# The path for splits with an expert over three tiles, under a second test in place of the other arm

## The chip, the cores and the metric

The kernel runs on one core of a Trainium2 chip. The metric is the device time of one execution in microseconds (us). The page of the profile gives, beside it, the span from the first to the last recorded instruction. The engines are PE (TensorE, matrix products; its weight loads stand as PEld), DVE (VectorE), ACT (ScalarE), POOL (GpSimd) and SP (SyncE, which here issues transfers). Each engine has a sequencer of its own, which reads the engine's instructions in order; the profile marks what the sequencer does itself (branches, semaphore instructions, drains) with a q: PEq or PEldq, DVEq, POOLq and so on.

## The reference

Sliding window attention for 8 batches of 8 heads, 576 positions and 64 dimensions, then a layer of 8 experts with one expert for each token:

```python
def _moe_ref(x, w_gate, w1, w2):            # x: 4608 x 512, from the attention
    logits = x @ w_gate                     # 512 x 8
    expert_idx = np.argmax(logits, axis=1)
    ...
    for e in range(E):                      # E = 8 experts
        lo, hi = (boundaries[e], boundaries[e + 1])
        h = np.maximum(x_sorted[lo:hi] @ w1[e], 0.0)     # 512 x 1024
        y_sorted[lo:hi] = h @ w2[e]                      # 1024 x 512
    y = y_sorted[inv_perm]
    return (gate_w[:, None] * y).astype(np.float32)
```

The number of tokens of an expert is known only when the kernel runs. For the given inputs the eight experts have 669, 400, 748, 505, 592, 390, 566 and 738 tokens.

## The kernel before

**Stages.** The first stage (lines 496 to 1044) is the attention, the choice of experts and the table `perm_i`, which holds for each slot of each tile the token that stands there. A tile is 256 slots (`TB`) of one expert. The last lines of this stage already work on the first two tiles of expert 0, and `loads()` (line 869) puts the numbers of tiles into registers of every engine: `regs[e]` for each expert, `end` (the number of all tiles) and `most` (the largest number of tiles of any expert). The second stage (from line 1054) works on the other tiles. The program is written in the order in which each engine is to run it, since both stages stand under `manual_schedule`.

**A tile.** `gather` fetches the rows of 256 tokens from `x_dram` by two indirect transfers that POOL issues. `hidden` multiplies by the first weights on PE, `output` by the second ones; both use seven products of halves in place of eight, with sums that DVE and POOL form. The last products of `output` write the PSUM banks that `yw2`, `yps[0]` and `yx2` name. `finish` (line 425) is the rest of a tile: three additions on DVE, through the helper `plus` on line 384, of which the first two read `yw2` and the third reads both halves of `yps[0]`. `scatter` (line 291) then sends the tile's 256 rows to their places in `out`: one small copy of the slots into `at_s` on POOL, then two indirect transfers of 256 KB each, `ys[1]` first and `ys[0]` after it. `finish` and `scatter` of a tile do not stand at its own end but at the start of the next one, in `body` (line 479), so that PE has work of the next tile meanwhile. After the last tile they stand by themselves, at line 1126.

**Branches.** `expert(e)` (line 1063) tests for each further tile whether the expert has it (line 1077, `tiles > n`) and whether it is a full one or one of at most 160 tokens (line 1078, `fulls > n`). It is written for at most three tiles of an expert (`KT`). `any_number` (line 1092) is a loop for any split: each turn loads the weights of its tile anew, forms all sums, gathers, multiplies and scatters. Line 1123 chooses between the two by `most`. With the tokens above no expert has more than three tiles, so that the arm with `expert` runs, and no instruction of the loop of line 1104 is in the trace. Each test is a compare and branch on every engine by itself.

**Semaphores.** Engines wait for each other by semaphores that count what an engine has finished; the waits compare with constants. Where two ways through the program come together, both must leave every count at the same value, so the framework puts an instruction into the way with fewer counts that waits for that engine's own last count and adds the difference (EVENT_SEMAPHORE in the rows; INC_SWDGE_SEM for those that POOL's indirect transfers count).

Of the kernel before, what the change touches and what calls it, by code (L numbers as in the profile page):

```python
# [11 lines left out]
F32 = mybir.dt.float32  # L12
# [3 lines left out]
ALU = mybir.AluOpType  # L16
AX = mybir.AxisListType
# [7 lines left out]
def _ins(ap: bass.AP, axis: int, n: int) -> bass.AP:  # L25

    dims = [list(d) for d in ap.ap]
    dims.insert(axis, [0, n])
    return bass.AP(tensor=ap.tensor, offset=ap.offset, ap=dims)


def _inner(ap: bass.AP, n: int) -> bass.AP:
    return _ins(ap, len(ap.ap), n)
# [3 lines left out]
def kernel(  # L37
# [11 lines left out]
    P = nc.NUM_PARTITIONS  # L49
    B, H, S, D = q.shape  # L50
    NT, DM = out.shape
    E = moe_w_gate.shape[1]
# [13 lines left out]
    C = TB // P  # L66
    NE = 2
    NTILE = (NT + TB - 1) // TB + E - 1 + NE
    NX = NTILE + 4
    NS = NX * C  # L70
    KT = 3
# [18 lines left out]
    perm_i = consts.tile([P, NS], I32, name="perm_i")  # L90
# [5 lines left out]
    expert_i = consts.tile([P, NTILE], I32, name="expert_i")  # L96
# [4 lines left out]
    V, G = nc.vector, nc.gpsimd  # L101
# [48 lines left out]
    def sums_w1(e):  # L150
        form(left_sums(G, s1s[e % NW], *w1q(e)))

    def sums_w2(e):
        form(right_sums(G, s2s[e % NW], *w2q(e)))

    def load_w1(e):
        return nc.sync.dma_start(out=w1s[e % NW][:], in_=w1v[e])

    def load_w2(e):
        nc.sync.dma_start(out=w2s[e % NW][:], in_=w2v[e])  # L160
# [7 lines left out]
    lane = consts.tile([P, P], BF16, name="lane")  # L168
# [9 lines left out]
    with tc.tile_pool(name="tmp", bufs=1) as tmp:  # L178
# [8 lines left out]
        for i in range(BG):  # L187
# [12 lines left out]
            out=before[:], in_=ones[:], pattern=[[1, P]], compare_op=ALU.is_gt, fill=0.0, base=0,  # L200
# [6 lines left out]
    nt, cum, start, chunk0 = (consts.tile([P, E], F32, name=n) for n in ("nt", "cum", "start", "chunk0"))  # L207
    rt = ctx.enter_context(tc.tile_pool(name="rt", bufs=1))
# [31 lines left out]
    v_m = Memory(consts.tile([P, 3 * 2 * BG * NV * 2 * VW], F32, name="v_m"))  # L240
# [27 lines left out]
    def form_all(parts):  # L268
        for _ in parts:
            pass  # L270

    def gather(tokens):
        G.tensor_copy(out=at_g[:], in_=tokens)
        for c in range(C):
            G.indirect_dma_start(  # L275
                out=xg[c], out_offset=None, in_=x_dram[:, :],
                in_offset=bass.IndirectOffsetOnAxis(ap=at_g[:, c : c + 1], axis=0),
            )
# [12 lines left out]
    def scatter(tokens):  # L291
        G.tensor_copy(out=at_s[:], in_=tokens)
        for c in reversed(range(C)):

            put = G.indirect_dma_start(  # L295
                out=out[:, :], out_offset=bass.IndirectOffsetOnAxis(ap=at_s[:, c : c + 1], axis=0),
                in_=ys[c], in_offset=None, bounds_check=NT - 1, oob_is_err=False,
            )
            tc.declare_no_dep(put.ins, group="puts", reason="every token has one slot, so no row is written twice")
            tc.add_to_no_dep_group("puts", put.ins)  # L300
# [24 lines left out]
    def keep_turned():  # L325
        for c in range(C):
            nc.scalar.copy(out=xq[:, :, c], in_=xn[:, c])  # L327

    def sums_x(src):

        b12, b22, b21 = src[1][:, 0:HG], src[1][:, HG:], src[0][:, HG:]
        for n, (a, b) in enumerate(((b12, part(0, 0)), (b22, xs[:, 0]), (b22, part(0, 1)), (xs[:, 1], b21))):
            V.tensor_tensor(out=xs[:, n], in0=a, in1=b, op=ALU.subtract)
# [91 lines left out]
    def finish():  # L425

        plus(ys[1][:, hi_], yw2, v3)
        plus(v2, yw2, v1)
        plus(ys[0], yps[0], v02)
# [49 lines left out]
    def body(e, last, after, full, between=None, next_x=True):  # L479

        finish()
        scatter(perm_i[:, last])
        if between is not None:
            between()
        blocks = turned_blocks() if next_x else iter(())
        if not full:
            half_tile(e, blocks, after, next_x)
            return
        form_all(hidden(e, blocks))
        parts = output(e, blocks, next_x)  # L490
        next(parts)
        if after is not None:
            gather(perm_i[:, after])
        form_all(parts)

    with tc.manual_schedule(), ExitStack() as held, ExitStack() as brief:
# [372 lines left out]
        def loads():  # L869

            _, n = nc.values_load_multi_w_load_instructions(info_i[0:1, :], min_val=0, max_val=NT // P)
            _, places = nc.values_load_multi_w_load_instructions(
                places_i[0:1, :], engines=(mybir.EngineType.Pool,), min_val=0, max_val=NTILE,
                skip_runtime_bounds_check_because="sums of numbers of tiles, at most NTILE for any tokens",
            )
            return [(n[e], n[E + e], places[e]) for e in range(E)], places[E], n[2 * E]
# [164 lines left out]
        regs, end, most = loads()  # L1041
# [12 lines left out]
    with tc.manual_schedule():  # L1054
        load_w1(1)
        load_w2(1)
        def at(n):
            n = nc.s_assert_within(
                n, 0, NTILE - 1, skip_runtime_bounds_check_because="a tile with a token is one of the NTILE"
            )  # L1060
            return lambda ahead: bass.ds((n + ahead) * C, C)

        def expert(e):

            fulls, tiles, first = regs[e]
            if 0 < e < E - 1:
                load_w1(e + 1)
                load_w2(e + 1)

            def one(n, full, between=None):  # L1070
                slots = at(first + n)
                ends = e == E - 1 and (n == KT - 1 or not full)
                body(e, slots(0), None if ends or e == E - 1 and n == KT - 2 else slots(3), full, between, not ends)

            def more(n, between=None):

                with tc.If(tiles > n) as some_left:  # L1077
                    with tc.If(fulls > n, preferred_fallthrough_block=False) as full:
                        one(n, True, between)
                        if n + 1 < KT:  # L1080
                            more(n + 1)
                    with full.Else():
                        one(n, False, between)
                if between is not None:
                    with some_left.Else():
                        between()

            if e:
                one(0, True, partial(sums_w2, e))
            more(1 if e else NE, partial(sums_w1, e + 1) if e + 1 < E else None)  # L1090

        def any_number():

            tiles_of = rt.tile([P, E, NTILE], F32, name="tiles_of")
            V.tensor_tensor(
                out=tiles_of[:], in0=_inner(cum[:], NTILE), in1=_ins(lane[:, 0:NTILE], 1, E), op=ALU.is_le
            )
            with nc.allow_low_precision("integers"):
                V.tensor_reduce(out=expert_i[:], in_=tiles_of[:].rearrange("p e t -> p t e"), axis=AX.X, op=ALU.add)
            _, (tiles,) = nc.values_load_multi_w_load_instructions(  # L1100
                places_i[0:1, E : E + 1], min_val=0, max_val=NTILE,
                skip_runtime_bounds_check_because="a sum of numbers of tiles, at most NTILE for any tokens",
            )
            with tc.For_i(NE, tiles) as i:
                _, (e,) = nc.values_load_multi_w_load_instructions(
                    expert_i[0:1, bass.ds(i, 1)], engines=(mybir.EngineType.SP,), min_val=0, max_val=E - 1,
                    skip_runtime_bounds_check_because="a tile that is numbered belongs to an expert",
                )
                for w, view in ((w1s[0], w1v), (w2s[0], w2v)):
                    nc.sync.dma_start(out=w[:], in_=view[bass.ds(e, 1)].rearrange("o p n d -> (o p) n d"))  # L1110
                sums_w1(0)
                sums_w2(0)
                slots = at(i)
                gather(perm_i[:, slots(1)])
                form_all(turned_blocks())
                keep_turned()
                sums_x([xn[:, c] for c in range(C)])
                form_all(hidden(0))
                form_all(output(0, iter(()), False))
                finish()  # L1120
                scatter(perm_i[:, slots(1)])

        with tc.If(most < KT + 1) as few:  # L1123
            for e in range(E):
                expert(e)
            finish()
            scatter(perm_i[:, bass.ds(end * C, C)])
        with few.Else():
            finish()
            scatter(perm_i[:, NE * C : (NE + 1) * C])  # L1130
            any_number()


# [26 lines left out]
```

## Time and profile before

| | |
|---|---|
| runs of the kernel | 721.09, 724.43, 720.25, 723.32 us; median 722.2 us |
| the profiled execution | 721.14 us, its span 719.4 us |
| mean granted clock of TensorE | 0.985 |
| PE busy, 290 to 700 us (second stage) | 408.85 of 410.00 us |
| PE busy, 700 to 719.4 us (the end) | 8.17 of 19.40 us |
| indirect transfers to `out` (line 295) | 42 on POOL, 1.0 us each to issue, median 3.2 us to landing |
| first and last entry of line 1123 | 249.5 us (SP) and 709.0 us (POOL) |

The profile is read on a page (busy time, slices, the chain of waits that ended last) and by questions to the trace: a timeline of the instructions in a stretch, merged where they are alike; and all instructions of one source line, with the shortest, the median and the longest duration in nanoseconds and the times of the first and the last one. A line of the timeline has the start, the duration until the last of the group ends, engine, source line, operation, what is written and read, how many, and in brackets the engine's idle time before it with what ended it. Matrix products are recorded with modelled ends.

### The profile page before, as it was taken

To read this page: it belongs to the slowest core of one execution; us is meant where nothing else is said; L and a number is where in the kernel's file an instruction comes from. 1 tells how busy PE (TensorE), PEld (TensorE's weight loads), DVE (VectorE), ACT (ScalarE), POOL (GpSimd) and SP (SyncE) were. 2 spreads that over 40 slices of the span, in tenths; PEclk is the share of its full clock that TensorE was granted. 3 is DMA by queue.
4 is the path that set the end of the run, shared out by engine and by line. 5 is a ranking of instruction groups with operands and counts; after the bars stand their busy time and mean duration, and the time that the engine had idled before them with its cause. 6 is when DMAs were issued, how large, how long until landed. Compare 5 with 4: busy or idle time off the path is not lost. (4 is left out here: it accounts for less than half of the span.)

```text
span 719.4 us, 17946 instructions
## 1 busy us (share of the span) xinstructions
PE 687.7 (96%) x6882; PEld 606.0 (84%) x6882; DVE 497.7 (69%) x1636; ACT 258.5 (36%) x653; POOL 350.8 (49%) x360
## 2 busy tenths in 40 slices
PE   4999999999979999999999999999999999999993
PEld 3888888878759898897999999899889799889993
DVE  3576899898966858676776686567756677766731
ACT  4688888878745111111121121122111112111110
POOL 4213749387474117857452446545265745272011
PEclk9899999999999999999999999999999999999997
DMA  8998889887442373617101631540361710111000
GB/s 158 221 203 183 178 197 234 205 205 197 123 159 92 104 260 128 215 59 263 51 30 62 199 115 39 192 148 15 124 210 59 269 50 25 61 37 61 2 31 28
DMA packets 137288, 93.37 MB, mean 130 GB/s; under 512 B 117008, under 2 KB 117008, under 8 KB 137170
## 3 DMA queue, kind: packets, MB, share of 16 engines
q1 hardware_dynamic: 127858, 62.16, 32.7%
q0 software_dynamic: 8736, 27.53, 11.8%
q10 hardware_dynamic: 576, 2.10, 1.0%
q8 instruction: 74, 1.21, 0.7%
q14 instruction: 44, 0.36, 0.2%
HBM read 72.89 MB, written 20.45 MB: 130 GB/s over the span
## 5 line engine op out<-in xcount | busy, mean ns | idle before, releaser
L315 DVE STREAM_TRANSPOSE v_m<-qk_m 32x256 f32<-32x256 f32 x304 | 132.4, 435 | 7.9 <-DMA qk_m<-x_dram,at_g 2.3
L344 PE MATMUL bank<-qk_m,s 128*128 128x128 f32 x1024 | 122.5, 275 | 0.2 <-DVE qk_m L365 0.2
L344 PEld LDWEIGHTS bank<-qk_m,s 128*128 128x128 f32 x1024 | 118.3, 192 | 0.4 <-issue 0.4
L275 POOL DMA_INDIRECT qk_m<-x_dram,at_g x38 | 41.0, 1080 | 141.3 <-DVE v_m L315 112.9
L651 ACT ACTIVATE pr<-pr,mx 128x128 f32<-128x128 f32 x288 | 89.6, 390 | 33.6 <-DVE mx L641 33.4
L344 PE MATMUL bank<-qk_m,w 128*128 128x128 f32 x768 | 93.8, 275 | 0.9 <-PEq L1077 0.7
L344 PEld LDWEIGHTS bank<-qk_m,w 128*128 128x128 f32 x768 | 90.6, 192 | 4.5 <-issue 4.1
L295 POOL DMA_INDIRECT out_dram<-v_m,at_s x42 | 42.5, 1011 | 87.5 <-DVE v_m L384 85.2
L641 DVE CUSTOM_DVE_ANT_0 pr<-bank,mask 128x128 f32<-128x128 f32 x288 | 64.3, 285 | 28.4 <-PE bank L628 27.1
L384 DVE TENSOR_TENSOR v_m<-bank,v_m 128x256 f32<-128x256 f32 (+1 forms) x95 | 43.8, 480 | 44.8 <-PE bank L388 30.1
L569 POOL COPY v_m<-v_m 64x520 f32<-64x520 f32 x32 | 19.8, 620 | 68.5 <-DMA v_m<-in_v_dram 58.3
L140 POOL TENSOR_TENSOR s<-w 128x1024 f32<-128x1024 f32 x22 | 52.2, 2374 | 0.0
L674 PEld LDWEIGHTS bank<-v_m,pT 128*64 128x64 f32 x1152 | 41.1, 140 | 11.9 <-DVE xs L688 5.8
L674 PE MATMUL bank<-v_m,pT 128*64 128x65 f32 x1152 | 47.8, 231 | 2.9 <-DVE xs L688 2.9
L351 ACT COPY qk_m<-bank 128x512 f32<-128x512 f32 x16 | 9.4, 587 | 108.7 <-PE bank L344 70.4
L388 PE MATMUL bank<-qkT_m,v_m 128*128 128x256 f32 x216 | 48.3, 379 | 0.0
L388 PEld LDWEIGHTS bank<-qkT_m,v_m 128*128 128x128 f32 x216 | 41.0, 190 | 5.5
L628 PE MATMUL bank<-qkT_m 64*64 64x128 f32 x1152 | 45.4, 287 | 0.2
L595 PE MATMUL bank<-ident,qk_m 128*128 128x128 f32 x256 | 36.8, 287 | 8.8 <-DMA qk_m<-in_q_dram 8.1
L444 PEld LDWEIGHTS bank<-qk_m,w 128*128 128x128 f32 x320 | 43.9, 190 | 0.9 <-issue 0.7
L444 PE MATMUL bank<-qk_m,w 128*128 128x160 f32 x320 | 44.4, 299 | 0.4 <-ACT qk_m L327 0.4
L659 PE MATMUL bank<-ident,pr 128*128 128x128 f32 x288 | 43.0, 287 | 0.0
(174 smaller groups left out, 1229.7 us busy)
## 6 DMA issues: line engine op xcount, KB each, us to landing
w<-in_moe_w_dram SPq DMA_DIRECT2D x11, 2048.0 KB, 9.8
qk_m<-in_q_dram SPq DMA_DIRECT2D x72, 128.0 KB, 3.9
qk_m<-in_k_dram SPq DMA_DIRECT2D x72, 128.0 KB, 3.7
v_m<-in_v_dram SPq DMA_DIRECT2D x64, 128.0 KB, 4.2
qk_m<-in_moe_w_dram SPq DMA_DIRECT2D x3, 2048.0 KB, 10.4
x_dram<-xs POOLq DMA_DIRECT2D x6, 512.0 KB
x_dram<-xs POOLq DMA_DIRECT2D x3, 768.0 KB
w<-in_moe_w_dram ACTq DMA_DIRECT2D x4, 512.0 KB, 4.4
```

Of the source, the lines that this page charges most:

```text
L140: op()
L295: put = G.indirect_dma_start(out=out[:, :], out_offset=bass.IndirectOffsetOnAxis(ap=at_s[:, c : c + 1], axis=0), in_=ys[c], in_offset=None ...
L315: V.transpose(out=xn[b * QD : (b + 1) * QD, :, :, a * QD : (a + 1) * QD].rearrange("p c g i -> p (c g) i"), in_=rows[a * QD : (a + 1) * QD ...
L344: nc.tensor.matmul(acc[:, f, :], lhsT=a[:, g, f * P : (f + 1) * P], rhs=b[:, g, :], start=(first and f == 0 and g == 0), stop=(g == HG - 1 ...
L384: plus = lambda out, a, b: V.tensor_tensor(out=out, in0=a, in1=b, op=ALU.add)
L388: nc.tensor.matmul(acc, lhsT=a[:, f, :], rhs=b[:, f, :], start=(start and f == 0), stop=(stop and f == HF - 1), skip_group_check=True,)
L444: nc.tensor.matmul(acc[:, i], lhsT=w1[:, g, f * P : (f + 1) * P], rhs=xq[:, g].rearrange("p c s -> p (c s)")[:, 0:HALF], start=(i + g == 0 ...
L628: nc.tensor.matmul(out_, lhsT=qT[rows, t, a * WINDOW : (a + 1) * WINDOW], rhs=rhs, start=True, stop=True, skip_group_check=True,)
L641: V.tensor_tensor_reduce(out=prs[h][:, m, :], in0=scs[h][:, m, :], in1=mask[:, m0 + m, :], scale=-scale, scalar=-2 * MASKED, op0=ALU.add, ...
L651: nc.scalar.activation(out=y, in_=y, func=AF.Exp, scale=-1.0, bias=mx[:, h, m : m + 1])
L659: nc.tensor.transpose(out=tr[:, m, :], in_=prs[h][:, m, :], identity=ident[:])
L674: nc.tensor.matmul(px[a * D : (a + 1) * D, h, m, :], lhsT=pTs[h][:, m, a * D : (a + 1) * D], rhs=vt[:, h, :], start=True, stop=True, skip_ ...
```

## The change

`any_number` no longer is the other arm of the first test. The first test has an arm only for splits of at most three tiles an expert. A second test, of the opposite sign, follows it and holds `any_number`; and `finish` and `scatter` of the last tile follow both tests, where both arms had a `finish` and a `scatter` of their own before. In the loop of `any_number`, `finish` and `scatter` of the tile before move from the end of a turn to its start. The table `tiles_of`, which only `any_number` uses, is no longer a tile of 864 bytes a partition in the pool `rt` but a view of the memory `v_m`.

```diff
-            tiles_of = rt.tile([P, E, NTILE], F32, name="tiles_of")
+            tiles_of = v_m(2080, E, NTILE)
...
                 slots = at(i)
+                finish()
+                scatter(perm_i[:, slots(0)])
                 gather(perm_i[:, slots(1)])
                 form_all(turned_blocks())
                 keep_turned()
                 sums_x([xn[:, c] for c in range(C)])
                 form_all(hidden(0))
                 form_all(output(0, iter(()), False))
-                finish()
-                scatter(perm_i[:, slots(1)])
-
-        with tc.If(most < KT + 1) as few:
+
+        with tc.If(most < KT + 1):
             for e in range(E):
                 expert(e)
-            finish()
-            scatter(perm_i[:, bass.ds(end * C, C)])
-        with few.Else():
-            finish()
-            scatter(perm_i[:, NE * C : (NE + 1) * C])
+        with tc.If(most > KT):
             any_number()
+        finish()
+        scatter(perm_i[:, bass.ds(end * C, C)])
```

More of the change, by code (lines that the diff above doesn't have):

```diff
@@ L1092, in any_number @@
         def any_number():
-            tiles_of = rt.tile([P, E, NTILE], F32, name="tiles_of")
+            tiles_of = v_m(2080, E, NTILE)
             V.tensor_tensor(
-                out=tiles_of[:], in0=_inner(cum[:], NTILE), in1=_ins(lane[:, 0:NTILE], 1, E), op=ALU.is_le
+                out=tiles_of, in0=_inner(cum[:], NTILE), in1=_ins(lane[:, 0:NTILE], 1, E), op=ALU.is_le
             )
             with nc.allow_low_precision("integers"):
-                V.tensor_reduce(out=expert_i[:], in_=tiles_of[:].rearrange("p e t -> p t e"), axis=AX.X, op=ALU.add)
+                V.tensor_reduce(out=expert_i[:], in_=tiles_of.rearrange("p e t -> p t e"), axis=AX.X, op=ALU.add)
             _, (tiles,) = nc.values_load_multi_w_load_instructions(
```

## The prediction

> **What bounds the kernel now.** I read the page first: PE works for nearly the whole span, so what counts is what PE waits for, and the piece at the end in which nothing is left for it.
>
> ```profile
> span 719.4 us, 17946 instructions
> ...
> PE 687.7 (96%) x6882; PEld 606.0 (84%) x6882; DVE 497.7 (69%) x1636; ACT 258.5 (36%) x653; POOL 350.8 (49%) x360
> ```
>
> The change moves nothing before the last tile of expert 7, so the next view is the timeline of the end.
>
> ```profile
> 706.28 1.89 PE L388 MATMUL bank<-w,v_m 128*128 128x256 f32 x8
> 706.54 0.76 DVE L384 TENSOR_TENSOR v_m<-bank,v_m 128x256 f32<-128x256 f32 x2 [0.90 <-PE bank L388]
> ...
> 707.75 0.98 POOL L295 DMA_INDIRECT out_dram<-v_m,at_s  x1 [19.93 <-DVE v_m L384]
> 708.21 0.69 DVE L384 TENSOR_TENSOR v_m<-bank,v_m 128x512 f32<-128x512 f32 x1 [0.92 <-PE bank L388]
> ...
> 709.18 0.98 POOL L295 DMA_INDIRECT out_dram<-v_m,at_s  x1 [0.45 <-POOLq L1123]
> ```
>
> The last product runs until 708.17. The first two additions of `finish` start at 706.54, beside it; only the third, at 708.21, needs its end. The first scatter has therefore been issued before the second half is added. After 709.18 there is one thing left, in the rows of line 1155:
>
> ```profile
> L1155 POOLq DRAIN  x3: 46/113/9387, 709.2 to 719.1; - x3
> L1155 SPq DRAIN  x3: 7/7/13, 712.8 to 718.8; - x3
> ```
>
> SP has seen all landings by 712.8; POOL's drain starts at 709.2, with the last scatter, and lasts 9.39 us, and the program ends 0.8 us after it.
>
> Then the branches: the rows of line 1123, and those of line 1077, where an expert with two tiles skips its third.
>
> ```profile
> L1123 PEldq COMPARE_BRANCH  x2: 95/1694/3292, 269.1 to 704.5; - x2
> ...
> L1123 POOLq COMPARE_BRANCH  x2: 37/40/44, 273.3 to 709.0; - x2
> L1123 DVEq COMPARE_BRANCH  x2: 47/54/60, 275.4 to 708.3; - x2
> ```
> ```profile
> L1077 PEldq COMPARE_BRANCH  x14: 68/75/4120, 269.3 to 679.5; - x14
> ...
> L1077 POOLq INC_SWDGE_SEM  x1: 1387/1387/1387, 452.9 to 452.9; - x1
> L1077 DVEq EVENT_SEMAPHORE  x1: 21/21/21, 455.1 to 455.1; - x1
> L1077 PEldq EVENT_SEMAPHORE  x1: 51/51/51, 457.8 to 457.8; - x1
> ...
>   DVE v_m L384: 2.8, 1
> ```
>
> On line 1123 the first branch is the test, the second the jump over the other arm at the end: 3.29 us on PE, some 0.05 on DVE and POOL. The rows of line 1077 hold one skipped body, with the semaphore instructions that make up its counts, and DVE's `finish` waits 2.8 us for PE there. What follows such a skip is what the change will put at the end:
>
> ```profile
> 455.71 1.89 PE L388 MATMUL bank<-w,v_m 128*128 128x256 f32 x8
> 457.90 1.54 DVE L384 TENSOR_TENSOR v_m<-bank,v_m 128x256 f32<-128x256 f32 x3 [2.83 <-PEq L1077]
> ...
> 459.16 1.02 POOL L295 DMA_INDIRECT out_dram<-v_m,at_s  x1 [4.21 <-DVE v_m L384]
> ...
> 460.49 1.00 POOL L295 DMA_INDIRECT out_dram<-v_m,at_s  x1 [0.30 <-issue]
> ```
>
> All three additions run in one piece, after the last product and after PE's semaphore instruction. At 706.54 two of them ran beside it.
>
> **The change part by part.** Removed: the jump over the other arm behind the last scatter, 0.04 us on POOL at 709.0. Nothing waits for it; worth nothing.
>
> Moved: the whole last step, that is three additions on DVE, one copy into `at_s`, the register moves and two indirect transfers on POOL. It moves past the second test on every queue. ACT and SP pass it at once and nobody waits for them: SP's last branch now is at 569.4. POOL's queue has nothing between 687.8, after the copy into `at_s`, and 707.0. It gets the test (0.04), some waits for landed transfers and an INC_SWDGE_SEM (1.39; 1.00 and 1.78 are the other rows); the copy slips from 687.6 to about 689.5, and 17 us of idle time hide that. Without this cover it would cost its 2 us whole.
>
> Added, and on the path: PE's test of `most > KT`, which jumps over the loop's body, then PE's instruction that makes up the counts. `finish` must wait for the count that holds on both ways, so all three additions wait for this instruction, as at 457.90. On DVE itself the jump costs 0.05 (rows above), and DVE is idle from 705.63 to 706.54 anyway.
>
> How late is PE's instruction? Now its sequencer starts the jump at 704.5 and is done 3.29 us later, at 707.8, under matrix products that run until 708.17. The new jump starts after one more short branch (0.07 to 0.34), and skips the same body: one full tile, 168 products and as many weight loads. It ends between 707.89 and 708.16, just under the products still. So PE's end decides, 708.17.
>
> The sum: from the start of PE's semaphore instruction (457.8 in its row, its own 0.05 included) to DVE's first addition at 457.90 it was 0.15 at most: first addition at 708.32. From there the distances of 457.90: first scatter 1.26 later, 709.58; second 1.33 after that, 710.91. Now it is 709.18: **1.73 us later**. Behind it wait SP's last waits and the drain. If the drain is counted from the last scatter or its landing, all of it moves: 721.14 + 1.73 = 722.87 against the profiled execution. That one lies 1.06 below the median of the runs, which is what a new median compares with: 722.2 + 1.73 = **723.9 us**.
>
> Bounds of what the trace does not show. The drain: it moves by 0, if something else sets its end, or by 1.73; its start row (0.01 after the last scatter's) speaks for the second, which I take. PE's jump: 0.07 at least; at most 6.41, the longest branch of line 1078:
>
> ```profile
> L1078 PEldq COMPARE_BRANCH  x19: 67/342/6412, 269.4 to 704.1; - x19
> ```
>
> That one came while weights were loaded, jumping over several bodies; the nearest row, same body and same moment, is 3.29. Moving `tiles_of` shifts later tiles by 864 bytes: no row shows that an address matters (products of line 344 last 275 ns from `s` and from `w`), and `any_number` does not run. Zero.
>
> A rule of the Trainium skill speaks against this step. The row first: 3.29 us for PE's jump, 0.05 for DVE's. The page "Runtime: NRT & Kernel Launch", section "Instruction fetch mechanics", says that a taken branch to code outside the fetched window stops execution until it has come; it gives no time for that. By that rule alone, with the stall wholly on the path, the sum would be 1.73 + 3.29 = 5.0 and the time 727.2; by the rows it is hidden under the products.
>
> **The rivals.** First, no added wait: the framework keeps the exact count for `finish`, and the two additions still run beside the last product. For it: at the joins near 290 and 331 two additions of `finish` start at 290.19 and 330.80, beside the products of line 470 that end at 291.40 and 334.09. Against it: there the way taken was the one with the products, and at 457.90, as here, it was not. Time 722.2, not slower.
>
> Second, clearly slower: the new jump takes as long as the 6.41 row. From 704.7 it ends at 711.1, 2.9 after PE's end; the sum is 1.73 + 2.9 = 4.6 and the time 726.8. It decides as soon as the jump takes over 3.5 us. Against it: the 3.29 at the same place. A join at which all engines wait for each other can't be its cause: at one test ACT branches at 677.5 and DVE at 680.6.
>
> Third, faster: POOL now jumps at 709.0, just before its drain. If the drain's length comes from that jump, with the code in one line it shrinks at most to the landing, 712.8 in place of 718.6: 5.8 less, 1.73 more, 718.1. Against it: POOL's jumps last 0.04, and the drain starts 0.15 after this one.
>
> Fourth, that the change does nothing here, since the loop does not run: only where its code's place and counts don't matter; the time is that of the first.
>
> **How the numbers follow.** Likeliest case 0.70; no added wait (with the fourth) 0.11; long jump 0.13; shorter drain 0.06. The predicted time is 723.9. The runs shown spread by 2 us to either side of their median, so I let a median move by 1: the low end is 722.2 - 1 = 721.2, which leaves out the short drain; the high end is 726.8 with 0.3 of that: 727.1. A change of 0.5% is 3.6 us, about what a measurement of this kernel can tell from none: faster is under 718.6, the third rival, 0.06; slower is over 725.8, the second rival and the likeliest case on a bad median, 0.13 + 0.08 = 0.21; the rest 0.73.
>
> **What would show it.** Right: the three additions of `finish` in one piece from about 708.3, after an idle time that PE's sequencer ends at the line of the second test; on that line a PE branch of about 3.3 us and one EVENT_SEMAPHORE each on PE, DVE and ACT, an INC_SWDGE_SEM on POOL near 688; the scatters at about 709.6 and 710.9; a drain of about 9.4 us; everything before 704 unchanged. Wrong: two additions still at 706.5 (first rival), a PE branch past 708.2 (second), a drain well under 9 us (third), or any shift before 700, which nothing here explains.

## The result, and the profile after

The changed kernel has a median of 723.19 us (52 runs) against 721.48 us (78 runs of the kernel before). The ratio is 1.0027, with a 95% interval from 1.0017 to 1.0036: slower by 1.95 us by this ratio, between 1.2 and 2.6 (the medians themselves differ by 1.71). The forecast was 1.73 us.

The profiled execution of the changed kernel has a span of 725.9 us, 6.5 more than that of before. Most of this is not the change. SP's first branch, which ends the first stage, lies at 249.5 us in the profile of before and at 254.0 in this one, and from there to the end of the last matrix product it is 458.6 and 458.9 us. In the ten profiled executions of this study that first branch lies anywhere between 249.5 and 254.0, and not by kernel: a second profile of the changed kernel has it at 250.3. So the two ends are compared from the last product on. The timeline of the changed kernel's end:

```profile
711.04 1.89 PE L388 MATMUL bank<-w,v_m 128*128 128x256 f32 x8
713.11 1.54 DVE L384 TENSOR_TENSOR v_m<-bank,v_m 128x256 f32<-128x256 f32 x3 [2.72 <-PEq L1126]
714.34 0.98 POOL L295 DMA_INDIRECT out_dram<-v_m,at_s  x1 [21.73 <-DVE v_m L384]
715.63 0.99 POOL L295 DMA_INDIRECT out_dram<-v_m,at_s  x1 [0.30 <-issue]
```

The last product ends at 711.04 + 1.89 = 712.93. All three additions of `finish` now come in one group behind it, at 713.11, where two of them stood beside the product before; what ended DVE's idle time is PE's sequencer on line 1126, the second test. The second scatter starts 715.63 - 712.93 = 2.70 after the product's end (2.71 from the unrounded times); before it was 709.18 - 708.17 = 1.01. The rows of the second test, and those of the program's end, now on line 1154:

```profile
L1126 PEldq EVENT_SEMAPHORE  x2: 51/51/51, 713.0 to 713.1; - x2
...
L1126 POOLq INC_SWDGE_SEM  x1: 2180/2180/2180, 689.8 to 689.8; - x1
...
L1126 PEldq COMPARE_BRANCH  x1: 3482/3482/3482, 709.1 to 709.1; - x1
L1126 DVEq COMPARE_BRANCH  x1: 63/63/63, 710.2 to 710.2; - x1
...
  DVE v_m L384: 2.7, 1
```
```profile
L1154 POOLq DRAIN  x3: 46/113/10342, 714.7 to 725.6; - x3
L1154 SPq DRAIN  x3: 7/7/13, 719.1 to 725.3; - x3
```

PE's jump over the loop starts at 709.1 and lasts 3.48 us, to 712.62, still 0.3 us under the product. PE's semaphore instruction follows at 713.0, and DVE's additions at 713.11. POOL's drain is recorded as longer (10.34 us for 9.39), but it starts at 714.7, 0.9 us before the second scatter; from that scatter's start to the end of the span it is 725.89 - 715.63 = 10.26, and 719.42 - 709.18 = 10.24 before. The drain has moved as a whole, and it goes by the issue of the last scatter, not by its landing: in the ten profiles the end lies 10.23 to 10.26 us behind the issue, and 7.24 to 7.52 behind the landing.

The chain of waits that ended last, in order of time, reaches back to DVE's wait and no further:

```profile
713.03 0.04 DVEq L384
713.07 0.04 issue
713.11 0.44 DVE v_m L384
...
714.34 0.98 POOL out_dram L295
715.33 1.29 POOLq L1154
```

### The profile page after: what moved, and what is told of

Its sections match the earlier page's. It is cut to its first block, busy times and chain, and to the rows that moved or that the text cites. A ratio compares the mean times of both kernels' runs of the same rounds, so it can differ in the third digit from the quotient of the medians.

```text
span 725.9 us, 17956 instructions
## 1 busy us (share of the span) xinstructions
PE 689.7 (95%) x6882; PEld 607.3 (84%) x6882; DVE 497.8 (69%) x1636; ACT 258.4 (36%) x653; POOL 350.8 (48%) x360
```

## The experiments

**Theory and rivals.** The theory is that the last additions wait for the instruction with which PE makes up the counts of the skipped loop, that this instruction can run only behind PE's last product, and that the price of 1.7 us is the lost overlap. The rivals: the price is PE's jump itself; it is the move of `tiles_of` and of all tiles behind it; a common end behind a second test costs in itself, whatever is waited for.

All eight experiments stand in one table, below the kernel before and the changed one. The ratio is to the kernel before. The three columns after it are read from each profile and count from the end of the last product, in us: start of the first of the last three additions, start of the second scatter, end of the span. The last column is PE's branch at the test or join where the loop is passed.

| kernel | ratio, 95% interval | first addition | second scatter | end | PE's branch |
|---|---|---|---|---|---|
| before | 1 | -1.63 | 1.01 | 11.25 | 3.29 |
| changed | 1.0027, 1.0017 to 1.0036 | 0.18 | 2.71 | 12.96 | 3.48 |
| changed, once more | 1.0018, 0.9995 to 1.0040 | 0.18 | 2.70 | 12.96 | 3.40 |
| tests swapped | 1.0055, 1.0035 to 1.0076 | -1.63 | 1.01 | 11.24 | 0.37 |
| short body | 1.0027, 1.0010 to 1.0045 | 0.18 | 2.71 | 12.96 | 0.35 |
| long body | 1.0024, 1.0008 to 1.0040 | 0.19 | 2.71 | 12.96 | 3.36 |
| table back | 1.0018, 1.0001 to 1.0035 | 0.18 | 2.71 | 12.96 | 3.60 |
| other arm kept | 1.0004, 0.9987 to 1.0021 | -1.63 | 1.00 | 11.25 | 3.49 |
| additions in the arms | 1.0015, 0.9992 to 1.0038 | -1.63 | 2.94 | 13.19 | 3.45 |
| two additions in the arms | 1.0007, 0.9987 to 1.0027 | -1.63 | 1.34 | 11.59 | 3.79 |

The ratios are known to some 0.2%, which is the size of the effect; the columns from the profiles agree to 0.02 us where the kernels should, and decide. Three ratios lie below or at the low end of what was expected (table back, additions in the arms, changed once more), though their intervals reach it; the ratio of the swapped kernel lies clear above.

**A shorter jump.** Of the changed kernel:

```diff
-                form_all(hidden(0))
                 form_all(output(0, iter(()), False))
```

> The changed kernel without hidden in the loop of any_number, which does not run with these tokens (the loop's arithmetic is incomplete, the output of this run is not touched by it): 224 PE instructions fewer to jump over. Wait theory: PE's jump at the second test falls from 3.5 us to under 0.5 us, PE's make-up instruction still waits for the last product, the three additions still run in one piece; the ratio stays at 1.0025 to 1.003. Fetch rival (the price is the jump): 1.000 to 1.0005.

PE's branch fell to 0.35 us and nothing else moved: the same 12.96 us, ratio 1.0027. The rows of the second test in this kernel, on its line 1125, show that PE still waits for its products before the semaphore instruction:

```profile
L1125 PEldq EVENT_SEMAPHORE  x2: 51/51/51, 712.2 to 712.4; - x2
...
L1125 PEldq COMPARE_BRANCH  x1: 347/347/347, 708.4 to 708.4; - x1
```

The branch is done at 708.8, the semaphore instruction comes at 712.2, when the last product (end 712.20) is. The price is not the jump. The Trainium skill, page "Runtime: NRT & Kernel Launch", section "Instruction fetch mechanics", says that a taken branch to code outside the fetched window waits for that code. That 224 PE instructions fewer take 3.1 us from the branch would fit this, but no run here shows what lay in the window. What the rows do show is that a branch of 3.48 us which ends before the queued products do costs nothing.

**A longer jump.** `form_all(hidden(0))` stands four times in the loop:

```diff
                 form_all(hidden(0))
+                form_all(hidden(0))
+                form_all(hidden(0))
+                form_all(hidden(0))
                 form_all(output(0, iter(()), False))
```

> The changed kernel with hidden four times in the loop that does not run: 672 PE instructions more to jump over. Wait theory with its cover of 3.5 us: if the jump takes 6.1 to 6.7 us, as the longest ones of line 1078, the end comes 2.6 to 3.2 us later than in the changed kernel, ratio 1.006 to 1.007; if the length of the jump does not matter beyond the next blocks of code and it stays at 3.5 us, 1.0027. Fetch rival: the whole jump counts, 1.008 or more.

The jump stayed at 3.36 us, the end at 12.96. So 672 instructions more do not by themselves make a jump as long as the branches of 6 us on line 1078, and the case that should have shown the cover run out (the 3.5 us and more for which the products queued ahead keep PE busy) did not come about in this kernel. The trace of before has it at another place, a branch of line 1078 between two tiles (its row, then the products around it):

```profile
L1078 PEldq COMPARE_BRANCH  x1: 4080/4080/4080, 379.4 to 379.4; - x1
```
```profile
381.39 1.89 PE L388 MATMUL bank<-qk_m,v_m 128*128 128x256 f32 x8
383.55 2.05 PE L344 MATMUL bank<-qk_m,w 128*128 128x128 f32 x16 [0.27 <-issue]
```

The branch lasts until 383.50, the products queued ahead of it until 381.39 + 1.89 = 383.28, and PE stands still until 383.55. The ten profiles hold eleven such branches behind the same cover of 3.9 us: after the shortest, 3.86 us, PE is idle for 0.02 us, after the longest, 4.17 us, for 0.34. So a stall is paid as far as it outlasts the products.

**The table back.**

```diff
-            tiles_of = v_m(2080, E, NTILE)
+            tiles_of = rt.tile([P, E, NTILE], F32, name="tiles_of")[:]
```

> The changed kernel with tiles_of in its own tile again, so that later tiles lie where they lay before. Wait theory: the move of the table is worth nothing, ratio 1.0025 to 1.003 as the changed kernel. Memory rival (the shift by 864 bytes is what costs): 1.000.

12.96 us again. The move of the table is worth nothing.

**All but the second test.**

```diff
-        with tc.If(most < KT + 1):
+        with tc.If(most < KT + 1) as few:
             for e in range(E):
                 expert(e)
-        with tc.If(most > KT):
+            finish()
+            scatter(perm_i[:, bass.ds(end * C, C)])
+        with few.Else():
             any_number()
-        finish()
-        scatter(perm_i[:, bass.ds(end * C, C)])
+            finish()
+            scatter(perm_i[:, bass.ds(end * C, C)])
```

> All of the change but the second test: any_number with its turned loop and its table in v_m as the other arm of the first test, finish and scatter written in both arms. Wait theory: as before, two additions beside the last product, ratio 0.999 to 1.001. Memory rival: 1.0025 to 1.003.

The end is that of before to 0.01 us, with the turned loop and the moved table in it, and PE's jump of 3.49 us too. The price belongs to the second test with a common end behind it, and to nothing else in the change.

**The additions in the arms.** `finish` moves into both tests, the scatter stays behind them:

```diff
         with tc.If(most < KT + 1):
             for e in range(E):
                 expert(e)
+            finish()
         with tc.If(most > KT):
             any_number()
-        finish()
+            finish()
         scatter(perm_i[:, bass.ds(end * C, C)])
```

> Both tests, finish inside the experts' arm and inside the loop's arm, only the scatter common behind them. The additions keep their old times, the third ends some 0.7 us after the last product; but the scatters now wait for the instruction with which DVE makes up its counts, behind the third addition. Wait theory, for whichever engine's make-up instruction: the first scatter is issued some 0.8 us after that instruction, the second 1.33 us after the first, so the second comes 1.9 to 2.1 us later than before: ratio 1.0025 to 1.003. Rival, only PE's instruction matters: the time of before, 1.000 to 1.0005.

```profile
706.97 0.76 DVE L384 TENSOR_TENSOR v_m<-bank,v_m 128x256 f32<-128x256 f32 x2 [0.90 <-PE bank L388]
708.64 0.69 DVE L384 TENSOR_TENSOR v_m<-bank,v_m 128x512 f32<-128x512 f32 x1 [0.91 <-PE bank L388]
710.25 0.98 POOL L295 DMA_INDIRECT out_dram<-v_m,at_s  x1 [21.81 <-DVEq L1127]
711.54 0.99 POOL L295 DMA_INDIRECT out_dram<-v_m,at_s  x1 [0.30 <-issue]
```

This is the timeline of its end. The additions have the distances of before, and yet the second scatter comes 1.93 us later than before, later even than in the changed kernel: POOL now waits for DVE's sequencer on line 1127, the second test, and DVE's instruction there stands behind the third addition:

```profile
L1127 DVEq EVENT_SEMAPHORE  x2: 21/21/21, 709.4 to 709.5; - x2
```

The wait is not PE's in particular. It is for the make-up instruction of whichever engine is waited for behind the skip.

**Two additions in the arms.** `plus(ys[1][:, hi_], yw2, v3)` and `plus(v2, yw2, v1)` stand inside both tests, `plus(ys[0], yps[0], v02)` and the scatter behind them:

```diff
         with tc.If(most < KT + 1):
             for e in range(E):
                 expert(e)
+            first_two()
         with tc.If(most > KT):
             any_number()
-        finish()
+            first_two()
+        plus(ys[0], yps[0], v02)
         scatter(perm_i[:, bass.ds(end * C, C)])
```

> Both tests, the first two additions of finish inside either arm, the third addition and the scatter common behind them. Wait theory: the two additions run beside the last product again; the third waits for PE's make-up instruction, 0.1 us later than before; the first scatter waits for DVE's make-up instruction, which comes early; the second scatter is at most 0.4 us later than before: ratio 1.000 to 1.001. Rival, a common end behind a second test costs in itself: 1.0025 to 1.003.

```profile
707.74 0.76 DVE L384 TENSOR_TENSOR v_m<-bank,v_m 128x256 f32<-128x256 f32 x2 [0.90 <-PE bank L388]
709.40 0.98 POOL L295 DMA_INDIRECT out_dram<-v_m,at_s  x1 [20.19 <-DVEq L1131]
709.75 0.69 DVE L384 TENSOR_TENSOR v_m<-bank,v_m 128x512 f32<-128x512 f32 x1 [1.25 <-PEq L1131]
710.72 0.98 POOL L295 DMA_INDIRECT out_dram<-v_m,at_s  x1 [0.33 <-DVE v_m L384]
```

The last product ends at 709.38 here. Two additions are beside it again, and the end is 0.34 us later than before, where the changed kernel is 1.71 later. What is left is the third addition, 0.37 after the product in place of 0.04: it waits for PE's make-up instruction, and that came late, because PE's jump was the longest of all here:

```profile
L1131 PEldq EVENT_SEMAPHORE  x2: 51/51/51, 709.7 to 709.8; - x2
...
L1131 PEldq COMPARE_BRANCH  x1: 3786/3786/3786, 705.8 to 705.8; - x1
```

The jump ends at 709.60, 0.23 us behind the last product. So in this kernel, at the very place of the change, a part of the jump is paid: the addition is 0.19 us later than in the changed kernel (0.37 against 0.18). A common end behind a second test costs little in itself; what costs is that waits which were for one exact result before are now for an engine's make-up instruction.

**The tests swapped.**

```diff
+        with tc.If(most > KT):
+            any_number()
         with tc.If(most < KT + 1):
             for e in range(E):
                 expert(e)
-        with tc.If(most > KT):
-            any_number()
         finish()
         scatter(perm_i[:, bass.ds(end * C, C)])
```

> The two tests in the other order: the loop's test first, the experts' test second, finish and scatter still common behind both. The way that runs is now the one with the experts last, so the counts behind it are exact. Wait theory (the last additions wait for the instruction with which PE makes up the counts of the skipped loop): that instruction now stands near 270 us, the first two additions run beside the last product again, the first scatter 1.4 us before the second; at most 0.7 us is paid near 270, as at the skip near 458; ratio to before 1.000, at most 1.001. Rival, a common end behind any second test costs in itself: ratio stays 1.0025 to 1.003.

The end came back in full (11.24 us, additions at -1.63), with `finish` and `scatter` still common behind two tests: the way that runs is now the one whose counts are exact there, that is, the waits are for the results themselves and not for a make-up instruction. But the kernel is the slowest of all, 1.0055. The expectation of at most 0.7 us near 270, ratio at most 1.001, was wrong in size. The timeline of PE there, first the swapped kernel, then the one before:

```profile
272.95 1.89 PE L388 MATMUL bank<-qk_m,v_m 128*128 128x256 f32 x8
277.77 2.41 PE L444 MATMUL bank<-qk_m,w 128*128 128x160 f32 x16 [2.92 <-DVEq L1123]
```
```profile
271.27 1.89 PE L388 MATMUL bank<-qk_m,v_m 128*128 128x256 f32 x8
273.53 4.72 PE L444 MATMUL bank<-qk_m,w 128*128 128x160 f32 x33 [0.36 <-ACT qk_m L327]
```

The skip of the loop now stands between two tiles. PE's first product of the next tile needs a copy of ACT and nothing of DVE that is late, and so it waited 0.36 us; behind the skip its wait for DVE is on the count that DVE makes up, and DVE does that at 277.5, after seven additions and subtractions of the tile before:

```profile
L1123 DVEq EVENT_SEMAPHORE  x2: 21/21/21, 277.5 to 277.6; - x2
```

PE waits 2.92 us, 2.56 more. From SP's first branch to the last product's end it is 461.5 us against 458.2 to 458.9 in the other nine profiles, so the profile shows 2.6 to 3.3 us of loss; the ratio says 4.0 us, with an interval from 2.5 to 5.5, from eight runs. It is the same mechanism with another engine's instruction, in a place where PE pays.

**The changed kernel once more.**

> The changed kernel once more, beside the three others on the same chip: ratio 1.0017 to 1.0036, the interval that it had; the profiled end from the last branch of line 1078 on PE to the last instruction 17.0 us, as in the first profile (15.3 us in the kernel before).

12.96 us from the last product, 2.70 to the second scatter; from the last branch of line 1078 on PE to the end it is 17.0 us, 15.3 before. The ratio was 1.0018 this time, its interval just reaching 1.

## Why the prediction was right

- **The place.** It said that the change is worth something only behind the last product. Shown: with the first stage's spread left aside, the time from the second stage's start to the last product is 458.6 us before and 458.9 after, and the difference lies at the end, 11.25 against 12.96 us.
- **The wait.** All additions in one piece behind PE's make-up instruction. Shown by the group at 713.11 and by the kernel that kept the other arm.
- **The sum.** First addition 0.15 after the product: measured 0.18. First scatter 1.41 after it: 1.42 (714.34 - 712.93 = 1.41 by the timeline's decimals). Second scatter 2.74: 2.71. In all 1.73 us: 12.96 - 11.25 = 1.71. The distances from the one skip in the trace of before held to 0.03 us.
- **PE's jump.** Foretold 3.3 us and hidden; 3.48 and hidden. The short body shows that it is not paid. There was some luck in this: the sum had the jump start 3.30 to 3.57 us before the last product's end and end 0.01 to 0.28 before it. The make-up instruction of line 1123 that stood ahead of PE's jump at 704.4 was no longer there, and the jump started 3.79 us before and ended 0.31 before; started as foretold, its 3.48 us would have ended between 0.09 before the product's end and 0.18 behind it. In the kernel with two additions in the arms the jump was not hidden whole.
- **The drain.** Taken to move whole; in all ten profiles 10.23 to 10.26 us lie between the second scatter's start and the end. The third rival (the jump of POOL makes the drain long) is out, since the changed kernel has no jump there.
- **What was off.** INC_SWDGE_SEM took 2.18 us, above the 1.00 to 1.78 of its other rows, and started 3 us sooner than foretold against the last product. The copy into `at_s` was to slip by 2 us and did not: it stands 20.5 us before the last product's end in both kernels, because it waited for landings anyway. Both lie in POOL's idle time. PE, DVE and ACT have two EVENT_SEMAPHOREs each at the second test, where one was foretold. A shift before 700 was named as a sign of being wrong, and this profile has one of 4.5 us; it lies ahead of the second stage, where executions of the changed kernel differ among themselves. The base was off by more: the median of 4 runs before was 722.2, that of 78 is 721.48, so the foretold 723.9 was 723.2 on the better base, and 723.19 was measured. That they agree so closely is chance: by its interval the ratio leaves the loss open between 1.2 and 2.6 us.
- **The first rival**, exact counts behind the skip, is out by the same group of three; **the second**, a jump that outlasts the products, by 3.48 and by the long body's 3.36, though its rule held, that it decides once the jump takes longer than the cover: two additions in the arms show it with 3.79; **the fourth**, no effect, by the end's 1.71 us, which every profile of the changed kernel has.

No version here beats the kernel before. The best one with a common end, two additions in the arms, lies 0.34 us behind it by its profile.

## What to carry to other kernels

An arm that is skipped can cost more than its compare and jump: where two ways join in this program, each engine has to bring its counts to the same value, behind all that it has still to do, and whoever waits for that engine behind the join waits for this in place of the one result that it needs. So in this kernel the way that runs is best the one whose counts are exact behind the join, and work that overlaps the end of that way best stands inside it. Before such an instruction is put elsewhere, look which engine is late there: at the end the skip cost 1.7 us, between two tiles it cost 2.6.

## What the runs showed that I had not expected

The swapped kernel's loss, above: a make-up instruction on DVE that held up PE for 2.92 us though PE needed nothing from the additions before it.

The jump's length did not grow with the distance (3.36 us over 672 PE instructions more, 3.48 over the plain body), and it was not set by the body that is skipped either: in the swapped kernel the jump over the same body took 0.37 us. Jumps on line 1078 take 5.8 to 6.9 us in every profile. Why those are longer, and what sets the length of a jump, stays open; no idle time of PE over 0.1 us follows the ones of 5.8 to 6.9 us, where those of about 4 us on the same line leave PE idle for up to 0.34.

The executions differ by up to 4.5 us before the second stage begins, two of the same kernel by 3.7, and by under 1 us from there to the last product where the order of the tests is the same. A profile of one execution each would have shown a loss of 6.5 us, nearly four times the real one.
